# Moving steps between slots in a two-level Strassen kernel: attention's first products behind the copy of kv, sums of x earlier, last output chunk in other PSUM banks, one division into block 1

## The chip, the cores and the metric

The kernel runs on one core of one Trainium2 chip. The metric is the device time of one execution in microseconds. Timed runs have no profile; a profiled execution gives the instruction times that are read here. All data are float32.

## What is computed

A linear attention without softmax, a normalisation over each head, and a two-layer network with a leaky ReLU:

```python
kv  = einsum('bhsd,bhse->bhde', k, v)          # 8 batches, 8 heads, 576 rows, 64 wide
o   = einsum('bhsd,bhde->bhse', q, kv)
rms = sqrt(mean(o * o, axis=-1) + 1e-6)
x   = (o / rms * g_norm)                       # to (8*576, 8*64) = (4608, 512)
h   = x @ w_in                                 # (4608, 2048)
g   = maximum(0.01 * h, h)
out = g @ w_out                                # (4608, 512)
```

## The kernel before

The 4608 rows are worked in nine blocks of 512, and d_ff = 2048 in four chunks c of 2 x 256. Block 0 multiplies plainly. Block 1 uses one level of Strassen's seven products (in the Winograd form, in the order 1, 2, 6, 5, 7, 3, 4) for h and for the output. Blocks 2 to 8 use two levels for h (49 small products of 128x128) and one level for the output. The sums of the weights that the products need are made in blocks 0 and 1, kept in DRAM and read back; the sums of x and of g are made as the blocks go.

**Slots.** From block 1 on, a block is 28 slots, `slot = 7 * c + t`. A slot puts one outer product of h on TensorE (seven inner products, in banks `ha` and `hb` for one half of the inner products and `hc`, `hd` for products 2, 5, 3 of the outer level), then an attention step if the slot has one, then one product of the output (banks `oa` for products 1, 6, 7, 4 and `oc` for 2, 5, 3). The output runs two slots behind (`LAG = 2`), so slot 23 holds outer product 6 of chunk 3's h and product 1 of chunk 2's output. In `oa`, product 4 of one chunk is followed a slot later by product 1 of the next. Banks accumulate: after each product the bank is added to an SBUF tile by VectorE or copied by ScalarE (`done`), and only then may the next product write it.

**After the seventh product of h** (`product_h_two`): seven adds on VectorE make g11, g21, g22, g12 from `qa` and `qc`, four ReLUs on ScalarE (`relu`), and four sums of g on POOL (`sums_of`, in the order s1, s3, s2, s4), which the output's products 5, 7, 6, 3 need.

**Sums of x** (`sides_x`): four sums on VectorE (`sums`: t1, t2, t3, t4), then inner sums on POOL (`inner(0)`, `inner(1)`, `inner(2)`), for the next block.

**Attention** of batch i + 1 is made in block i, a step at a time (`attention`, a generator). With `fine` its 21 steps are: six for turning q and the products of kv, with q, k, v of later batches put in the load queue; one for `copy_kv` (PSUM to SBUF); and then two tails, one for the rows of the batch that end block i + 1 and one for those that begin block i + 2. A tail (`tail_of`) is: products with kv for e = 0, squares and copies on ScalarE; the same for e = 1, with two adds on VectorE; and `divide` in five steps (turn and reduce for l = 0; the same for l = 1 and the root; reciprocal and spread; turn back and multiply, twice). `FINE_SLOTS` says how many steps each slot takes, and `LATE_SLOTS` (3, 4) that the last two steps of the second tail run in the next block. Attention of batch 1 runs in block 0 with coarser steps, at the places in `steps`. Blocks 7 and 8 have no attention steps of their own; blocks 2 to 7 make sums of x for the block after.

**Order.** TensorE, transfers, and in blocks 2 to 8 VectorE's instructions are pinned to the order in which the program issues them (`pin`, `in_turn`); other instructions are placed by a scheduler. SyncE issues the loads, ScalarE the stores.

Of the kernel before, what the change touches and what calls it, by code (L numbers as in the profile page):

```python
# [23 lines left out]
def kernel(  # L24
# [46 lines left out]
    NB = B * S // NT  # L71
    N2 = NT // 2
    U = 2
    NC = DF // 2 // (U * P)
# [42 lines left out]
    def matmul(*args, **kw):  # L117
        pin(nc.tensor.matmul(*args, **kw))  # L118
# [462 lines left out]
    def add(eng, out_, a, b_, minus=False, pinned=False):  # L581
        ins = eng.tensor_tensor(out_, a, b_, op=ALU.subtract if minus else ALU.add)  # L582
        if pinned or steady and eng is nc.vector:
            pin(ins)
# [88 lines left out]
    def w_place(n):  # L673
        return view(w1_all, n % RING * NG, 7, P)
# [60 lines left out]
    def strassen(tags, left, right, done):  # L735


        banks = {}
        for i in ORDER:
            b = tags[0 if i in (1, 6, 7, 4) else 1]  # L740
            if i in FRESH:
                banks[b] = ps_m.tile([P, 2, N2], F32, tag=b, name=f"{b[0]}_{b[1]}")
            bank = banks[b]
            for part in range(2):
                for r in range(2):
                    matmul(bank[:, part, :], lhsT=left(i, part, r), rhs=right(i, part, r),
                           start=i in FRESH and part == 0 and r == 0, stop=(r == 1),
                           skip_group_check=True)
            done(i, bank.rearrange("p u (v n) -> p (u v) n", v=2))
            yield  # L750
# [4 lines left out]
    def g_of(c):  # L755


        return [view(g_all[c % 2], 0, 4, 4, P)[:, :, i, :] for i in range(4)]
# [40 lines left out]
    def product_h_two(i, c, quarters, to):  # L799

        n0 = 7 * ((i - 2) * NC + c)

        into = {1: (0, True), 2: (0, False), 6: (1, True), 5: (3, True), 7: (3, False),
                3: (1, False), 4: (2, True)}
        banks = {}
        for t, k in enumerate(ORDER):
            for js, tags, q in zip(GROUPS, (("ha", "hc"), ("hb", "hd")), (qa, qc)):
                tag = tags[0 if k in (1, 6, 7, 4) else 1]
                if k in FRESH:
                    banks[tag] = ps_m.tile([P, len(js), P], F32, tag=tag, name=f"h_{tag}")  # L810
                for n, j in enumerate(js):
                    matmul(banks[tag][:, n, :], lhsT=w_place(n0 + t)[:, AT[j], :],
                           rhs=quarters[k][j], start=k in FRESH and n == 0, stop=True,
                           skip_group_check=True)
                at, fresh = into[k]
                if fresh:
                    nc.scalar.copy(q[:, at], banks[tag])  # L817
                else:
                    add(nc.vector, q[:, at], banks[tag], q[:, at])
            read(n0 + t + 1 + RING)  # L820
            yield
        g11, g21, g22, g12 = g_of(c)
        add(nc.vector, g21, qa[:, :, 0, :], qa[:, :, 1, :])
        add(nc.vector, g11, qa[:, :, 0, :], qc[:, :, 0, :])
        yield
        add(nc.vector, g22, g21, qa[:, :, 2, :])
        add(nc.vector, g12, g22, qa[:, :, 3, :])
        add(nc.vector, g22, g22, qc[:, :, 1, :])
        add(nc.vector, g21, g21, qc[:, :, 1, :])
        add(nc.vector, g21, g21, qc[:, :, 2, :])  # L830
        for t in (g11, g12, g22, g21):
            relu(t)
        sums_of(c, to)

    def product_o(n, g_sides, os, finish):
        c = n % NC
        w_sides, _ = sides_w2(n)
        sums = sides_w2(n + 1)[1] if n + 1 < NC * (NB - 1) else lambda i: None
        if c == 0:
            for key in ("11", "12", "21", "22"):  # L840
                os[key] = opool.tile([P, 2, N2], F32, tag="o", name=f"o{key}", bufs=6)

        into = {1: ("11", True), 5: ("22", True), 2: ("11", False), 6: ("12", True),
                3: ("12", False), 7: ("22", False), 4: ("21", True)}

        def done(i, bank):
            key, fresh = into[i]
            to = os[key].rearrange("p u (v n) -> p (u v) n", v=2)
            if c == 0 and fresh:
                nc.scalar.copy(to, bank)  # L850
            else:
                add(nc.vector, to, bank, to)
            if c == NC - 1 and i in (2, 7, 3, 4):
                finish(key, os[key])

            if i == 5:
                sums(0)
            elif i == 4:
                sums(1)

        yield from strassen(("oa", "oc"), lambda i, part, r: g_sides[i][:, 2 * r + part, :],
                            lambda i, part, r: w_sides[i][:, r, :], done)

    def go(steps, n=None):
        while n is None or n > 0:
            if next(steps, steps) is steps:
                return
            n = None if n is None else n - 1
# [9 lines left out]
    def first_block(between):  # L878
# [26 lines left out]
        for t in range(4):  # L905
# [3 lines left out]
            else:  # L909
# [2 lines left out]

    first_attention()
    steps = {i: tail for tail in [tail_of(0, NT, S)] for i in (6, 8, 10)}
    steps.update((i, a1) for a1 in [attention(1, False)]
                 for i in (12, 13, 15, 16, 18, 20, 22, 23, 24, 26, 28, 29))
    loaded, rounded = 7, 5

    def between(n, half):
# [16 lines left out]
    x_sides, _, sums, _ = sides_x(1)  # L936
# [6 lines left out]
    for part in range(2):  # L943
# [1 line left out]

    A_SLOTS = (1, 3, 5, 8, 10, 11, 13, 14, 15, 17, 18, 19, 21)

    FINE_SLOTS = {1: 1, 2: 1, 4: 1, 9: 1, 10: 2, 11: 2, 12: 1, 15: 1, 16: 1, 17: 2, 18: 1, 19: 2,
                  22: 1, 24: 1, 25: 1}
    LATE_SLOTS = (3, 4)  # L950
    a_steps = iter(())

    LAG = 2
    o_queue, waited = collections.deque(), 0
# [1 line left out]
    def go_o():  # L956
        while o_queue:
            if next(o_queue[0], o_queue) is not o_queue:
                return True
            o_queue.popleft()  # L960

    for i in range(1, NB):
        one = i == 1
        steady = not one
        late, a_steps = a_steps, attention(i + 1, fine=not one) if i + 1 < B else iter(())
        os = {}
        for c in range(NC):
            g_sides = {}
            h_steps = product_h(c, h_sides, x_sides, g_sides) if one else \
                product_h_two(i, c, quarters, g_sides)  # L970
            for t in range(7):
                slot = 7 * c + t
                go(h_steps, 1)
                if not one:

                    if t == 6:
                        go(h_steps, 1)
                    if slot in LATE_SLOTS:
                        go(late, 1)
                    for _ in range(FINE_SLOTS.get(slot, 0)):  # L980
                        go(a_steps, 1)
                    if i + 1 < NB:
                        if slot == 22:
                            x_sides, new_quarters, sums, inner = sides_x(i + 1)
                        if slot in (22, 23, 24):
                            go(sums, 2 if slot == 23 else 1)
                        if slot == 24:
                            inner(0)
                        elif slot == 25:
                            inner(1)  # L990
                    load_some()
                if waited == LAG:
                    go_o()
                elif o_queue:
                    waited += 1
                if one:

                    if t == 1:
                        combine(c, 2)
                    if t == 3 and c < NC - 1:  # L1000
                        h_sides, more_h = sides_w1(c + 1)
                        combine(c + 1, 0)
                    if t == 5 and c < NC - 1:
                        more_h()
                        combine(c + 1, 1)
                    if slot in A_SLOTS:
                        go(a_steps, 1)
                    load_some()
                    if slot == 24:
                        go(a_steps)  # L1010
                        x_sides, new_quarters, sums, inner = sides_x(i + 1)
                        go(sums)
                    elif slot == 25:
                        inner(0)
                    elif slot == 26:
                        inner(1)
            go(h_steps)
            if c == NC - 1 and i + 1 < NB:
                inner(2)
                quarters = new_quarters  # L1020
            if one:
                read((2, 4, RING, RING)[c])
            o_queue.append(product_o((i - 1) * NC + c, g_sides, os, store(i)))
# [32 lines left out]
```

## Time and profile before

| | |
|---|---|
| median of 8 runs | 946.29 us (945.12 to 948.06) |
| the profiled execution | 947.4 us, span 945.7 us |
| mean granted TensorE clock | 0.996 |
| blocks 2, 3, 4, 5, 6 (237.7 to 739.3 us) | 100.3 us each |
| blocks 7, 8 | 92.1 us each |
| a plain slot | 3.29 us |

The span reaches from the first instruction to the last; about 1.7 us lie around it. In the rows of the timeline the columns are start, duration, engine, line, operation, output and inputs, shapes, count, and in brackets how long the engine had idled and what ended that. Busy time of a TensorE matmul is modelled, since matmuls are pipelined.

### The profile page before, as it was taken

The numbers are of one execution on the slowest core, as the hardware profiler recorded it, in microseconds if no ns is written. First come the engines' busy times: TensorE is split into PE (matmuls) and PEld (weight loads), VectorE is DVE, ScalarE is ACT, GpSimd is POOL, SyncE is SP. The second block draws the span as 40 slices with busy tenths as digits, with TensorE's granted clock in tenths as the row PEclk, the third lists the DMA queues.
The fourth block names the chain that finished last, engine by engine and source line by source line (L and its number), as shares of the span: only waits on it lengthen the run. The fifth ranks groups of instructions, "written<-read, shape, count | busy, mean of one in ns | idle before, by whom it ended". The sixth has DMA issues, their size and how long they took to land.

```text
span 945.7 us, 17997 instructions
## 1 busy us (share of the span) xinstructions
PE 924.0 (98%) x7076; PEld 781.1 (83%) x7076; DVE 610.9 (65%) x992; ACT 327.6 (35%) x659; POOL 320.6 (34%) x318
## 2 busy tenths in 40 slices
PE   7999999999999999999999999999999999999997
PEld 5544447878988899889988998899898999999996
DVE  2867894577456866587746874687558755754554
ACT  2543633241134322433244323432344233223321
POOL 2000353976622442226201722262224422532222
PEclk8999999999999999999999999999999999999999
DMA  7989915985498579855995589658655675567632
GB/s 249 220 228 232 256 63 189 292 294 162 147 331 261 173 202 299 265 170 182 280 280 178 181 237 300 208 176 246 229 182 167 201 220 181 182 196 222 189 110 83
DMA packets 90068, 200.05 MB, mean 212 GB/s; under 512 B 9857, under 2 KB 42113, under 8 KB 89985
## 3 DMA queue, kind: packets, MB, share of 16 engines
q1 hardware_dynamic: 79392, 186.85, 66.0%
q10 hardware_dynamic: 10144, 10.88, 3.4%
q8 instruction: 56, 0.92, 0.4%
q0 software_dynamic: 448, 1.18, 0.3%
q14 instruction: 28, 0.22, 0.1%
HBM read 172.39 MB, written 26.48 MB: 210 GB/s over the span
## 4 chain that ended last, share of the span: by engine, by line
PE 89%; DVE 6%; DMA 2%; issue 1%; ACT 0%; SPq 0%; POOL 0%; DVEq 0%; ACTq 0%; POOLq 0%
PE o_a L118 22%; PE o_c L118 18%; PE h_ha L118 10%; PE h_hc L118 8%; PE h_hb L118 7%; PE h_hd L118 6%; PE o_acc L118 4%; PE h_ps L118 4%; PE kv_ps L118 2%; PE o_ps L118 2%; PE h_a L118 2%; PE h_b L118 1%; PE h_c L118 1%; PE h_d L118 1%; DMA pairs<-in_v_dram 1%
## 5 line engine op out<-in xcount | busy, mean ns | idle before, releaser
L582 POOL TENSOR_TENSOR gs<-g 128x512 f32<-128x512 f32 x64 | 80.9, 1283 | 451.9 <-ACT g L753 451.9
L582 DVE TENSOR_TENSOR o<-o_c,o 128x512 f32<-128x512 f32 x88 | 60.6, 688 | 105.3 <-PE o_c L118 105.2
L582 DVE TENSOR_TENSOR o<-o_a,o 128x512 f32<-128x512 f32 x104 | 71.5, 688 | 86.2 <-PE o_a L118 86.2
L118 PE MATMUL o_a<-pairs,gs 128*128 128x256 f32 x512 | 121.6, 380 | 0.0
L753 ACT ACTIVATE g<-g 128x512 f32<-128x512 f32 x124 | 78.2, 631 | 116.5 <-DVE g L582 116.4
L817 ACT COPY w_all<-h_ha 128x512 f32<-128x512 f32 x84 | 48.7, 579 | 178.7 <-PE h_ha L118 176.0
L118 PEld LDWEIGHTS o_a<-pairs,gs 128*128 128x128 f32 x512 | 93.0, 190 | 11.9 <-issue 1.4
L118 PE MATMUL o_a<-w,g 128*128 128x256 f32 x256 | 61.6, 384 | 4.5 <-DVE o L582 4.5
L118 PE MATMUL o_c<-w,g 128*128 128x256 f32 x256 | 61.6, 383 | 0.0
L118 PE MATMUL o_c<-pairs,gs 128*128 128x256 f32 x256 | 61.6, 383 | 0.0
L118 PEld LDWEIGHTS h_ha<-stage,w_all 128*128 128x128 f32 x448 | 58.8, 192 | 2.9
L118 PE MATMUL o_a<-pairs,g 128*128 128x256 f32 x256 | 60.5, 379 | 0.0
L118 PE MATMUL o_c<-w,gs 128*128 128x256 f32 x256 | 60.5, 379 | 0.0
L118 PE MATMUL h_ha<-stage,w_all 128*128 128x128 f32 x448 | 59.0, 275 | 0.0
L118 PE MATMUL o_acc<-w,g 128*128 128x512 f32 x128 | 58.3, 598 | 0.7 <-ACT g L896 0.7
L118 PE MATMUL h_ps<-xT,w_all 128*128 128x512 f32 (+1 forms) x136 | 57.9, 570 | 0.2 <-DVE w_all L255 0.2
L582 DVE TENSOR_TENSOR g<-g,pairs 128x512 f32<-128x512 f32 x84 | 55.6, 689 | 1.9
L118 PEld LDWEIGHTS o_a<-w,g 128*128 128x128 f32 x256 | 46.4, 190 | 11.3 <-DVE o L582 3.4
L582 DVE TENSOR_TENSOR w_all<-h_hc,w_all 128x512 f32<-128x512 f32 x56 | 38.4, 686 | 25.4 <-PE h_hc L118 25.2
L582 POOL TENSOR_TENSOR pairs<-w_all 128x512 f32<-128x512 f32 x8 | 11.1, 1387 | 128.6 <-ACT cut L244 109.7
L118 PEld LDWEIGHTS o_c<-pairs,gs 128*128 128x128 f32 x256 | 46.4, 190 | 9.8 <-DVE inv L379 1.6
L118 PEld LDWEIGHTS o_c<-w,g 128*128 128x128 f32 x256 | 46.4, 190 | 8.6 <-issue 3.1
(188 smaller groups left out, 1964.3 us busy)
## 6 DMA issues: line engine op xcount, KB each, us to landing
w_all<-w SPq DMA_DIRECT2D x196, 448.0 KB, 4.1
pairs<-w SPq DMA_DIRECT2D x56, 512.0 KB, 4.4
out_dram<-o ACTq DMA_DIRECT2D x36, 256.0 KB, 4.5
v_in<-in_v_dram SPq DMA_DIRECT2D x29, 288.0 KB, 5.8
k_in<-in_k_dram SPq DMA_DIRECT2D x28, 288.0 KB, 5.9
q_in<-in_q_dram SPq DMA_DIRECT2D x56, 144.0 KB, 6.2
q_in<-in_q_dram SPq DMA_DIRECT2D x56, 140.0 KB, 5.8
w<-stage SPq DMA_DIRECT2D x12, 512.0 KB, 4.6
```

The lines of the kernel that those rows point to most:

```text
L118: pin(nc.tensor.matmul(*args, **kw))
L582: ins = eng.tensor_tensor(out_, a, b_, op=ALU.subtract if minus else ALU.add)
L753: nc.scalar.activation(t, t if src is None else src, func=AF.Prelu, alpha=SLOPE)
L817: nc.scalar.copy(q[:, at], banks[tag])
```

## The change

- `FINE_SLOTS`: attention's steps in blocks 2 to 6. Two steps shared slot 11 (the copy of kv and the first tail's products for e = 0); now slot 11 has the copy alone, slot 12 the e = 0 products and slot 15 those for e = 1, and the next two steps share slot 16. The second tail's e = 1 step goes from slot 19 to slot 23, and its three steps after that from 22, 24, 25 to 24, 25, 26.
- Sums of x start at slot 20 with two (before: slot 22 with one, then two, then one); the third comes in slot 21 and the fourth in slot 22. The inner sums on POOL stay at slots 24 and 25.
- The last chunk of the last block's output uses the banks `hd` and `hc` in place of `oa` and `oc`.
- `product_h_two` has one more place to pause; in the last chunk one step of the output is put there, between its second and third group of adds.
- The last step of batch 1's attention leaves block 0 and is issued in slot 4 of block 1, as the `late` part.

```diff
@@ product_h_two
         add(nc.vector, g22, g21, qa[:, :, 2, :])
         add(nc.vector, g12, g22, qa[:, :, 3, :])
+        yield
         add(nc.vector, g22, g22, qc[:, :, 1, :])
@@ product_o
-        yield from strassen(("oa", "oc"), lambda i, part, r: g_sides[i][:, 2 * r + part, :],
+        yield from strassen(("oa", "oc") if n + 1 < NC * (NB - 1) else ("hd", "hc"), lambda i, part, r: g_sides[i][:, 2 * r + part, :],
@@ block 0
-    steps.update((i, a1) for a1 in [attention(1, False)]
-                 for i in (12, 13, 15, 16, 18, 20, 22, 23, 24, 26, 28, 29))
+    a_steps = attention(1, False)
+    steps.update((i, a_steps)
+                 for i in (12, 13, 15, 16, 18, 20, 22, 23, 24, 26, 28))
@@ blocks 1 to 8
-    FINE_SLOTS = {1: 1, 2: 1, 4: 1, 9: 1, 10: 2, 11: 2, 12: 1, 15: 1, 16: 1, 17: 2, 18: 1, 19: 2,
-                  22: 1, 24: 1, 25: 1}
+    FINE_SLOTS = {1: 1, 2: 1, 4: 1, 9: 1, 10: 2, 11: 1, 12: 1, 15: 1, 16: 2, 17: 2, 18: 1, 19: 1,
+                  23: 1, 24: 1, 25: 1, 26: 1}
...
-    a_steps = iter(())
...
-                        if slot == 22:
+                        if slot == 20:
                             x_sides, new_quarters, sums, inner = sides_x(i + 1)
-                        if slot in (22, 23, 24):
-                            go(sums, 2 if slot == 23 else 1)
+                        if slot in (20, 21, 22):
+                            go(sums, 2 if slot == 20 else 1)
...
+                    if slot == 4:
+                        go(late, 1)
                     if slot in A_SLOTS:
...
+            if i == NB - 1 and c == NC - 1:
+                go(h_steps, 1)
+                go_o()
             go(h_steps)
```

## The prediction

> **What bounds the kernel now.** I read the page first, then TensorE's waits from the first two-level block on, then the length of every slot (one h product and one o product, with attention products in some), and last the other engines' timeline around the slots that are too long.
>
> ```profile
> span 945.7 us, 17997 instructions
> ...
> PE 924.0 (98%) x7076; PEld 781.1 (83%) x7076; DVE 610.9 (65%) x992; ACT 327.6 (35%) x659; POOL 320.6 (34%) x318
> ```
>
> TensorE is busy 98% of the span: only its holes can be won. Waits of TensorE from 237 to 945 us (total, times, longest):
>
> ```profile
> PE o_ps L118 <- DVE kv L321: 5.0, 5, 1.0
> PE o_a L118 <- DVE o L582: 4.5, 6, 2.1
> ```
>
> Five waits of 1.01 us are attention's first products waiting for the copy of kv, one in each of blocks 2 to 6. The o_a waits are five of 0.48 us in the same blocks and one of 2.07 us at the end. A hole costs more than its wait, so I take slot lengths, from one h product's start to the next. A plain slot is 3.29 us (417.88 to 421.17). In block 3, slots 11, 12, 22 and 23, of 28 counted from 0 (stretch, then length and busy times):
>
> ```profile
> 377.05:382.40 5.35, 4.34 (x39) 3.50 (x38) 2.32 (x5) 1.39 (x4) 0.00 (x0) 1.00 1.05 288
> 382.40:386.48 4.08, 4.08 (x40) 3.34 (x39) 1.99 (x4) 1.97 (x5) 0.00 (x0) 1.00 0.80 245
> 417.88:421.17 3.29, 3.29 (x24) 3.08 (x23) 3.22 (x7) 1.66 (x4) 1.50 (x2) 1.00 0.46 145
> 421.17:425.20 4.03, 3.55 (x23) 3.15 (x22) 4.03 (x5) 1.06 (x2) 3.95 (x3) 1.00 0.80 246
> ```
>
> Slots 11 and 12 hold equal attention products (64x256), yet differ by 1.27 us; over the five blocks the pairs are 5.46/4.18, 5.35/4.08, 5.25/3.97, 5.14/3.86 and 5.04/3.75: 6.40 us in all. Slot 23 holds no attention and is 4.03 or 4.04 instead of 3.29: 0.75 x 5 = 3.7 us. Why it is long (timeline):
>
> ```profile
> 420.90 1.26 POOL L582 TENSOR_TENSOR gs<-g 128x512 f32<-128x512 f32 x1
> ...
> 421.45 1.27 DVE L582 TENSOR_TENSOR xt<-xT 128x512 f32<-128x512 f32 x1
> 422.13 1.72 POOL L582 TENSOR_TENSOR gs<-gs,g 128x512 f32<-128x512 f32 x1
> ...
> 422.64 0.68 DVE L582 TENSOR_TENSOR o<-o_a,o 128x512 f32<-128x512 f32 x1
> ...
> 423.37 1.99 PE L118 MATMUL o_a<-w,g 128*128 128x256 f32 x8 [0.48 <-DVE o L582]
> ```
>
> VectorE's first sum of x takes 1.27 us, where it took 0.69 with POOL idle (225.85 us, block 1). It ends 0.55 us after POOL's second sum of g (its s3), and then comes the add that frees bank o_a. The same holds in all of blocks 2 to 6: it starts 0.85, 0.72, 0.59, 0.45 and 0.33 us before s3 ends and lasts 1.40, 1.27, 1.14, 1.00 and 0.87 us.
>
> **The change part by part.** In the changed program's instruction order, everything up to slot 11 of block 2 is the same on every engine, and SyncE's queue is the same throughout. Work, operations and transfers are unchanged.
>
> *Division into block 1.* The scheduler put that division's instructions at the same places before. Worth 0; no DMA moves.
>
> *First products a slot later.* The copy of kv stays in slot 11 (done 379.83), attention's e=0 products go to slot 12 (at 382.40 - 2.06 for the shorter slot 11 + 1.65 into the slot = 382.0): no wait can be left. The e=1 products go to slot 15. Slot 11 falls to 3.29: -(26.24 - 16.45) = -9.79; slot 12 keeps its length with the other half's products; slot 15 grows from 3.29 to slot 12's lengths, +(19.84 - 16.45) = +3.39. Sum **-6.40**. Behind the e=1 products ScalarE has two squares and two copies, then the copy of o_a that slot 16's product needs: from the products' start to the last copy 2.16 us (384.05 to 386.21), so until 3.8 us of slot 15. Bank o_a is filled at 4.2, its copy ends at 4.8, and slot 16 wants the bank at 5.6. Cover 0.8 us; if it is gone, 0.1 to 0.5 us a block.
>
> *Sums of x two slots earlier, and the second tail's e=1 products from slot 19 to slot 23.* In slot 20 VectorE now runs g21, g11 (413.07, 413.68), the first two sums at 414.29 and 415.01 (0.61 and 0.72 later, as in block 1), then the add of o at 415.62 instead of 414.79, since it had idled 0.42 us there. All after it is 0.83 us later: the last three g adds at 417.74, POOL's sums of g at 420.50, its s3 from 421.73 to 423.00. The third sum runs at 419.68 to 420.37, just ahead of POOL: no cost. But the fourth, in slot 22, starts at 419.68 + 0.61 + 0.60 + 0.59 + 0.47 = 421.95, inside s3. By the five rows it ends 0.55 after s3: 423.55. The add of o ends at 424.15, slot 23's o product starts at 424.20. So the same collision remains, with another sum, 0.83 us later. Slot 23 becomes 4.04 + 0.83 = 4.87; the attention products now in it (4.08 to 4.50 as slot lengths) fit in the hole. Slot 19 falls from 21.46 in total to 16.45. Sum over five blocks: +4.15 - 5.01 = **-0.86**. Block 7 has sums of x but no attention to fill the hole; its slot 23 was 3.29 and becomes 4.87: **+1.58**.
>
> Here a rule of the Trainium skill bears. *SBUF — State Buffer*, "Who interferes with whom": a VectorE instruction with two SBUF inputs contends with a GpSimd instruction that reads SBUF; the loser blocks until the other's whole instruction is over. The rows agree in kind. Taken at its worst (a whole POOL sum of 1.28 ahead of 0.69), the fourth sum would end at 423.92, 0.37 later: 6 x 0.37 = 2.2 us more. I keep the rows' 0.55.
>
> VectorE's two e=1 adds in slot 23 also meet POOL; even with a POOL sum of 1.28 each, the add of o after them is done by about 428.6 and bank o_a is wanted in slot 25, at 430.9. POOL's inner sums of x still wait for slot 24's products to leave their buffer, and POOL has room (34%). The second tail's turning and reciprocal move from slots 22, 24, 25 to 24, 25, 26, where the sums of x have left VectorE free.
>
> *Last chunk in banks of h, and the added yield.*
>
> ```profile
> 925.87 2.02 DVE L582 TENSOR_TENSOR g<-g,pairs 128x512 f32<-128x512 f32 x3
> ...
> 927.81 0.68 DVE L582 TENSOR_TENSOR o<-o_c,o 128x512 f32<-128x512 f32 x1
> ...
> 928.63 2.48 POOL L582 TENSOR_TENSOR gs<-g 128x512 f32<-128x512 f32 x2 [17.95 <-ACT g L753]
> ...
> 929.24 1.97 PE L118 MATMUL o_a<-w,g 128*128 128x256 f32 x8 [2.07 <-DVE o L582]
> ...
> 931.07 1.27 POOL L582 TENSOR_TENSOR gs<-gs,g 128x512 f32<-128x512 f32 x1
> ...
> 932.76 0.59 PE L118 MATMUL o_a<-pairs,gs 128*128 128x256 f32 x2
> ```
>
> The bank wait of 2.07 goes: products 1 and 2 can start at 927.01 and 928.74. Product 6 then wants POOL's s2 at 930.47. In the new order the o_c add stands ahead of the last three g adds: 0.60 later for them, for the ReLU, for POOL; s2 ends at 932.94 instead of 932.34. Product 6 starts about 933.0 instead of 932.76, plus 0.10 of restart (an o product after a wait takes 1.83, not 1.73): **+0.35**. No row shows how fast TensorE follows POOL; bounds -0.1 (it starts before POOL's recorded end) and +0.7; nearest is 0.05, its start after VectorE. A rule speaks otherwise: *Perfetto Trace Analysis*, "Optimizing Tensor Performance", wants independent groups in different PSUM banks so that evacuation overlaps the next matmuls; by it 2.2 us would be won here and the whole sum be -7.9. The rows say that POOL's chain ends last, so I take +0.35.
>
> **Sum:** -6.40 - 0.86 + 1.58 + 0.35 = -5.3 us against the profiled execution (947.4, span 945.7 and 1.7 around it). That run lies 1.1 above the median of eight, 946.29; holes in a program order do not depend on that, so I take the difference to the median: **941.0**.
>
> **The rivals.**
> *The fourth sum slips in ahead of s3.* It is only 0.22 us late for that (421.95 against 421.73). Then it ends by 422.6, the o product follows at 423.3, and slot 23 has no hole in blocks 2 to 6: -3.73 instead of -0.86, and block 7 pays 0.64: -6.40 - 3.73 + 0.64 + 0.35 = -9.1, **937.2**. Against it: both chains start from the same g add, so their distance is rigid. 0.13.
> *Partly eaten:* the skill's whole-instruction block, or slot 15's ScalarE cover gone: 1.5 to 2.5 us less, **942.5 to 943.5**. No row shows it. 0.09.
> *Slower: POOL takes the port twice.* If s2 goes before the waiting fourth sum, six slots 23 grow by another 1.28: 941.0 + 7.7 = **948.7**. It decides from 5.3/6 = 0.89 us a block. Against it: in all five rows VectorE went in after the instruction under way, and s2 was stretched to 1.72. With a few unforeseen queues at that place, 0.05.
> *No change* (the gain eaten in slots 20 to 23 almost exactly): 0.03.
>
> **How the numbers follow.** My case has 0.70, with its own range 939.9 to 942.2 (end bound, slot 15). To hold 8 in 10 the range takes in the early slip below and the eaten part above: 937.0 to 943.3. A difference of 0.2% (1.9 us) is about what a measurement of this kernel can tell from none. Faster by more: 0.70 + 0.13 + 0.09 = 0.92; within: 0.03; slower: 0.05.
>
> **What the changed profile would show.** Right: no wait of o_ps on kv; slot 11 at 3.29; slot 23 near 4.9 in blocks 2 to 7, with a wait of o_a on VectorE's o and a fourth sum of about 1.6 us that ends after s3; at the end no bank wait, but product 6 waiting for POOL's gs. Wrong: slot 23 at 4.1 to 4.5 (early slip), or over 5.7 (POOL twice); a new wait in slots 12, 15 or 16; a last product 6 that starts at once.

## The result, and the profile after

| | before | after |
|---|---|---|
| median | 946.65 us (32 runs, 944.72 to 948.37) | 942.38 us (11 runs, 940.53 to 944.69) |
| ratio, 95% interval | | 0.9957 (0.9949 to 0.9966) |
| the profiled execution | 947.4 us, span 945.7 | 943.18 us, span 941.5 |

The change makes the kernel 0.43% faster: 4.1 us (3.2 to 4.8 by the interval), where 5.3 were forecast. The difference is larger than the noise, and smaller than the forecast by more than the noise. The head of the page after:

```profile
span 941.5 us, 17989 instructions
...
PE 923.0 (98%) x7076; PEld 781.0 (83%) x7076; DVE 616.0 (65%) x992; ACT 327.1 (35%) x659; POOL 317.6 (34%) x318
```

VectorE is busy 5 us longer with the same 992 instructions: some of them now stand longer beside POOL. TensorE's waits from 237 to 945 us (total, times, longest):

```profile
PE o_a L118 <- DVE o L582: 4.1, 6, 1.3
PE h_d L118 <- POOL gs L582: 2.3, 1, 2.3
PE o_a L118 <- ACT o L851: 0.6, 1, 0.6
```

The five waits for the copy of kv are gone. Three others stand there instead: slot 23 (six times, the longest in block 7), product 6 of the last chunk behind POOL, and one on ScalarE, in block 6, which the forecast had named as a danger and put at nothing in its sum. The slots of block 3 that answer to those shown before, in the order 11, 12, 22, 23, then slot 23 of blocks 4 and 7 (stretch, length, busy times of TensorE, weight load, VectorE, ScalarE and POOL with the number of instructions, granted clock, busy share of the DMA engines, GB/s):

```profile
374.22:377.51 3.29, 3.29 (x24) 3.08 (x23) 2.31 (x5) 0.00 (x0) 0.00 (x0) 1.00 0.98 272
377.51:381.58 4.07, 4.07 (x39) 3.34 (x38) 1.23 (x2) 1.97 (x5) 0.00 (x0) 1.00 0.92 296
...
412.88:416.17 3.29, 3.29 (x24) 3.08 (x23) 3.22 (x6) 2.63 (x5) 0.33 (x1) 1.00 0.48 142
416.17:421.38 5.21, 4.25 (x39) 3.34 (x38) 5.21 (x7) 2.66 (x6) 5.13 (x4) 1.00 0.73 257
515.38:520.24 4.86, 4.36 (x39) 3.34 (x38) 4.67 (x6) 2.88 (x6) 4.78 (x4) 1.00 0.80 271
807.29:812.14 4.85, 3.56 (x23) 3.16 (x22) 2.96 (x4) 1.06 (x2) 4.76 (x4) 1.00 0.79 262
```

Slot 11 is plain. Slot 23 is 4.86 where the forecast had 4.87, and 5.21 in block 3. The timeline of block 4 shows the collision in its new place:

```profile
514.71 2.50 POOL L582 TENSOR_TENSOR gs<-g 128x512 f32<-128x512 f32 x2 [20.22 <-ACT g L753]
...
516.15 1.60 DVE L582 TENSOR_TENSOR w_all<-xT,w_all 128x512 f32<-128x512 f32 x1
517.17 1.72 POOL L582 TENSOR_TENSOR gs<-gs,g 128x512 f32<-128x512 f32 x1
517.68 0.68 DVE L582 TENSOR_TENSOR o<-o_a,o 128x512 f32<-128x512 f32 x1
...
518.41 1.99 PE L118 MATMUL o_a<-w,g 128*128 128x256 f32 x8 [0.50 <-DVE o L582]
```

POOL's s1 and s3 (first line) end at 517.21. The fourth sum of x (second line; in this block t4 lies in a `w_all` tile) starts inside s3 and ends about 0.55 us after it: it takes 1.60 us where 0.69 is its price alone, and the add that frees o_a can only follow it.

Slot lengths before and after, all blocks:

| slots | before | after | difference | forecast |
|---|---|---|---|---|
| 11, blocks 2 to 6 | 5.46, 5.35, 5.25, 5.14, 5.04 | 3.29 each | -9.79 | -9.79 |
| 15, blocks 2 to 6 | 3.29 each | 4.19, 4.08, 3.97, 3.87, 3.75 | +3.41 | +3.39 |
| 16, block 6 | 3.29 | 4.11 | +0.82 | 0 |
| 19, blocks 2 to 6 | 4.08, 4.19, 4.29, 4.40, 4.50 | 3.29 each | -5.01 | -5.01 |
| 23, blocks 2 to 6 | 4.04, 4.03, 4.04, 4.04, 4.04 | 4.86, 5.21, 4.86, 4.86, 4.86 | +4.46 | +4.15 |
| 23, block 7 | 3.29 | 4.85 | +1.56 | +1.58 |
| slot 0 of block 2 to slot 27 of block 8 | 682.53 | 677.98 | -4.55 | -5.68 |

Two parts of the span lie outside that table. The start, to slot 0 of block 2, is 1.58 shorter in the profile after (237.73 to 236.15). That is not the change. In both profiles the instructions of TensorE, VectorE, ScalarE and POOL come in the same order up to slot 11 of block 2. And over all the profiles of this document, the four with the division at its old place (before, and the three parts tried alone) have that slot at 235.7 to 237.7, on average 236.6, and the nine with the new place at 235.7 to 237.6, on average 236.8. The end, from slot 27 of block 8, is 1.93 *longer* (25.44 to 27.37), where +0.35 was forecast. Its rows, in stretches (columns as above):

```profile
924.33:926.74 2.41, 0.16 (x1) 0.00 (x0) 0.69 (x1) 0.00 (x0) 2.36 (x2) 1.00 0.23 81
926.74:928.50 1.76, 1.76 (x4) 1.49 (x5) 0.00 (x0) 0.00 (x0) 1.26 (x1) 0.51 0.11 38
928.50:930.26 1.76, 1.76 (x6) 1.37 (x6) 0.00 (x0) 0.00 (x0) 0.00 (x0) 0.52 0.00 0
930.26:931.98 1.72, 1.72 (x9) 1.52 (x8) 0.69 (x1) 0.00 (x0) 0.00 (x0) 1.00 0.00 0
```

Product 6 starts at 926.74, after 2.41 us without a product, and then runs at half the clock: 3.68 us instead of 1.9. Before, TensorE stood still for 2.23 us two products earlier, ahead of product 1, and went on at full clock. Whether the change causes that, or an execution happens to draw it, no single trace can tell.

### The profile page after: what moved, and what is told of

Its sections match the earlier page's. It is cut to its first block, busy times and chain, and to the rows that moved or that the text cites. A ratio compares the mean times of both kernels' runs of the same rounds, so it can differ in the third digit from the quotient of the medians.

```text
span 941.5 us, 17989 instructions
## 1 busy us (share of the span) xinstructions
PE 923.0 (98%) x7076; PEld 781.0 (83%) x7076; DVE 616.0 (65%) x992; ACT 327.1 (35%) x659; POOL 317.6 (34%) x318
## 3 DMA queue, kind: packets, MB, share of 16 engines
q0 software_dynamic: 448, 1.18, 0.3%
## 4 chain that ended last, share of the span: by engine, by line
PE 87%; DVE 8%; DMA 2%; issue 1%; POOL 1%; ACT 1%; SPq 0%; ACTq 0%; DVEq 0%; POOLq 0%
PE o_a L118 21%; PE o_c L118 17%; PE h_ha L118 10%; PE h_hc L118 8%; PE h_hb L118 7%; PE h_hd L118 6%; PE o_acc L118 4%; PE h_ps L118 4%; PE kv_ps L118 2%; PE o_ps L118 2%; PE h_d L118 2%; PE h_c L118 2%; PE h_a L118 1%; DMA pairs<-in_k_dram 1%; DVE o L582 1%
## 5 line engine op out<-in xcount | busy, mean ns | idle before, releaser
L582 DVE TENSOR_TENSOR o<-o_c,o 128x512 f32<-128x512 f32 x85 | 58.5, 688 | 108.2 <-PE o_c L118 108.1
L118 PE MATMUL o_a<-pairs,gs 128*128 128x256 f32 x496 | 117.3, 379 | 0.0
L582 DVE TENSOR_TENSOR o<-o_a,o 128x512 f32<-128x512 f32 x100 | 68.7, 687 | 71.1 <-PE o_a L118 71.0
L118 PEld LDWEIGHTS o_a<-pairs,gs 128*128 128x128 f32 x496 | 90.0, 190 | 9.9
L118 PE MATMUL o_c<-w,g 128*128 128x256 f32 x248 | 59.7, 383 | 0.0
L118 PE MATMUL o_c<-pairs,gs 128*128 128x256 f32 x248 | 59.2, 381 | 0.0
L118 PEld LDWEIGHTS o_a<-pairs,g 128*128 128x128 f32 x248 | 45.0, 190 | 6.5 <-DVE w_all L582 0.9
```

## The experiments

Each is a kernel with one edit, timed against the kernel before on the same chip. "Start to end" below is from slot 0 of block 2 to slot 27 of block 8, so it holds neither the start nor the end.

**The copy of kv alone** (in the kernel before):

```diff
-    FINE_SLOTS = {1: 1, 2: 1, 4: 1, 9: 1, 10: 2, 11: 2, 12: 1, 15: 1, 16: 1, 17: 2, 18: 1, 19: 2,
+    FINE_SLOTS = {1: 1, 2: 1, 4: 1, 9: 1, 10: 2, 11: 1, 12: 1, 15: 1, 16: 2, 17: 2, 18: 1, 19: 2,
```

> Only attention's first products are moved (e=0 from slot 11 to 12, e=1 from 12 to 15); sums of x, the last chunk's banks and the division stay as in the kernel before. If the forecast's first step holds: slot 11 at 3.29 in blocks 2 to 6 (-9.79), slot 15 at 4.19 to 3.75 (+3.4), and the ScalarE wait that the changed kernel showed in block 6 (0.8) may come back: -5.6 to -6.4, about 940.5 against 946.4. Slots 19 and 23 as in the kernel before. The rival, that the copy of kv was only hiding a later wait (ScalarE's copies in slot 15 in every block): -3 to -4, with a wait of o_a on ScalarE in slot 16 of all five blocks.

Measured: 941.82 us, ratio 0.9953 (0.9940 to 0.9965), so about -4.5 us; the median is 1.3 above the one expected. Start to end is -5.50, just short of what was expected: slot 11 falls to 3.29 to 3.35 in all five blocks, slot 15 is 4.18 to 3.76, and block 6's slot 16 is 4.12, +0.83. The wait on ScalarE in block 6 belongs to this part, then; blocks 2 to 5 have none. The profile's last chunk ran its product 1 at half clock (3.51 us), and two of the five executions had a mean granted clock of 0.995, where none of the 30 of the kernel before, timed beside them, was under 0.996. The three executions at 0.996 have a median of 941.52, the 19 of the kernel before at 0.996 one of 947.28: -5.8, near what the slots say. This part alone gives all of the gain.

**The sums of x and the second tail alone** (in the kernel before):

```diff
-... 18: 1, 19: 2, 22: 1, 24: 1, 25: 1}
+... 18: 1, 19: 1, 23: 1, 24: 1, 25: 1, 26: 1}
-                        if slot == 22:
+                        if slot == 20:
-                        if slot in (22, 23, 24):
-                            go(sums, 2 if slot == 23 else 1)
+                        if slot in (20, 21, 22):
+                            go(sums, 2 if slot == 20 else 1)
```

> Only the sums of x (slots 20 to 22) and the second tail's e=1 products (slot 19 to 23) are moved. The forecast's step: the fourth sum of x takes 1.6 us and ends 0.55 after POOL's third sum; slot 23 at 4.87 in blocks 2 to 6 (+0.83 each) and in block 7 (+1.58), slot 19 at 3.29 (-5.01): together +0.7, up to +1.1 with the odd longer slot of block 3, so about 947.2 (no gain). The rival, that moving the sums is what makes the changed kernel faster: -3 to -4, 942.5, with no hole in slot 23.

Measured: 948.30 us, ratio 1.0020 (1.0010 to 1.0030): a loss of 1.9 us (0.9 to 2.8). Start to end +0.99, slot by slot as in the table above (slot 23 at 4.85, 5.22, 4.86, 4.86, 4.86; block 7 4.84). The rival's gain is not there. The slots' +0.99 lies at the lower end of that interval. The rest lies with the clock: seven of the 17 executions had a mean clock under 0.996, where none of the 30 before had. At equal clock the medians differ by 0.9 (0.996: 948.15 of 7 and 947.28 of 19) and 1.3 (0.998: 946.98 of 3 and 945.68 of 11). Why this kernel had the low clock so often stays open.

**The end alone** (in the kernel before): the added `yield`, the banks `hd` and `hc`, and the o product put ahead.

> Only the last chunk's output goes to the banks of h, with the yield and the o add put ahead. POOL's chain ends last: product 6 waits 2.2 us for POOL's sums of g instead of 2.07 for the bank earlier. The forecast's +0.35 if TensorE then runs at full clock; +1.9 if the half clock (0.51) of the changed kernel comes back in product 6 after that wait. The rival (independent banks are won in full): -2.2.

Measured: 947.09 us, ratio 1.0007 (0.9997 to 1.0016): no difference that this can tell. TensorE's waits, in total, times, longest:

```profile
PE h_d L118 <- POOL gs L582: 2.2, 1, 2.2
```

Product 6 waits for POOL exactly as in the changed kernel, 12.61 after slot 27 in both, but here it runs at full clock, 2.00 us. From slot 27 to the end of the span it is 25.67, +0.23 to before. At equal clock the medians say the same: +0.2 at 0.998 (4 and 11 executions), +0.3 at 0.996 (9 and 19). So +0.35 was the right size; the other 1.7 of the profile after is the half clock, and the half clock does not always come. The -2.2 that the bank rule would have given did not come: the bank was free, and the product waited for its operand.

**Filling the gap.** Matmuls of 128x512 into bank oa between products 2 and 6, in the changed kernel, with results that are never read: five (below), and later two.

```diff
+            if i == 2 and n + 1 == NC * (NB - 1):
+                fill = ps_m.tile([P, NT], F32, tag="oa", name="fill_ps")
+                for _ in range(5):
+                    matmul(fill, lhsT=w2_sb[0][c][:, 0, :P], rhs=w2_sb[0][c][:, 0, :], start=True, stop=True)
```

> The changed kernel with five matmuls of 128x512 added into bank oa, between the last chunk's output products 2 and 6; their result is never read. They shorten the idle stretch of TensorE there from 2.4 us to about 1.2. If the idle stretch is what halves the clock: product 6 starts at the same distance behind POOL and takes 1.9 us instead of 3.7, so -1.75 against the changed kernel (940.7). If the half clock has another cause (the last work of the kernel, POOL's traffic, the length of the run): no change, or the half clock stays.

Measured: 943.26 us, ratio 0.9967 (0.9955 to 0.9979). I had sized it badly: the five took 4.45 us, not 1.2, so product 6 started 14.49 after slot 27 instead of 12.61. It ran at full clock (1.89), and what was won so was lost by the later start.

> The changed kernel with two matmuls of 128x512 (1.8 us by the 4.45 of the five tried) in the gap ahead of the last chunk's product 6; their result is never read, and product 6 starts as before, 12.6 after slot 27. If an idle TensorE is what halves the clock there: never a halved product 6, so no execution at a mean clock of 0.994, and a median 0.5 to 1.7 below the changed kernel's 942.4. If the halving has another cause, executions at 0.994 go on turning up and the median stays.

Measured: 942.68 us, ratio 0.9958 (0.9946 to 0.9971). Two took 1.88, product 6 started 12.62 after slot 27 and ran 1.99, and none of five executions had a mean clock of 0.994 (four of twelve of the changed kernel had). But the expected lower median did not come: four of the five had 0.996, as with two half-clock stretches at the start. As a test of the cause by the time it is inconclusive.

**The fourth sum of x early** (in the changed kernel):

```diff
-                        if slot in (20, 21, 22):
-                            go(sums, 2 if slot == 20 else 1)
+                        if slot in (20, 21):
+                            go(sums, 2)
```

> The changed kernel, with the third and the fourth sum of x both in slot 21, so that the fourth is done before POOL's third sum of g starts. If slot 23's hole is that one collision: slot 23 is as long as its attention products need (4.08 to 4.50 instead of 4.86, and 5.22 in block 3), about -3.2 in blocks 2 to 6, and about -0.9 in block 7: 938.3 against 942.4 for the changed kernel. If another instruction of VectorE takes the fourth sum's place behind POOL, or the add of o is late for another reason, slot 23 stays near 4.86 and the time near 942.4.

Measured: 938.17 us, ratio 0.9914 (0.9902 to 0.9927). Slot 23 is 4.08, 4.30, 4.29, 4.39, 4.50, and 3.92 in block 7; start to end -4.01 against the changed kernel. Block 4 in its timeline:

```profile
513.86 0.68 DVE L582 TENSOR_TENSOR w_all<-xT,w_all 128x512 f32<-128x512 f32 x1
514.08 2.83 POOL L582 TENSOR_TENSOR gs<-g 128x512 f32<-128x512 f32 x2 [20.23 <-ACT g L753]
...
516.12 0.68 DVE L582 TENSOR_TENSOR o<-o_a,o 128x512 f32<-128x512 f32 x1
516.87 1.26 POOL L582 TENSOR_TENSOR gs<-gs,g 128x512 f32<-128x512 f32 x1
```

The fourth sum (first line) takes 0.68, the o_a add is done before POOL's s2 (last line) starts, and TensorE waits for neither. So the hole of slot 23 in blocks 2 to 6 was that one collision. In block 7 0.63 of 1.56 remain, with a wait of 0.4 for the o_a add.

**The root a slot later** (in the changed kernel). The step that moves holds one turn and one reduce on VectorE, and the root on ScalarE:

```diff
-    FINE_SLOTS = {... 15: 1, 16: 2, 17: 2, 18: 1, 19: 1,
+    FINE_SLOTS = {... 15: 1, 16: 1, 17: 3, 18: 1, 19: 1,
```

> The changed kernel, with the second half of the sums' turning and the root of attention's division in slot 17 instead of 16, so that in block 6 ScalarE copies bank o_a ahead of the root. If the 0.55 wait in block 6 comes from that order: slot 16 of block 6 at 3.29 again, -0.82 and nothing else. If the division is then late for the second tail's products: a new wait or longer slots from 18 on, and no gain.

Measured: 941.88 us, ratio 0.9949 (0.9937 to 0.9962). Block 6's slot 16 is 3.29 again (-0.82), and slot 23 of block 3 is 4.86 instead of 5.21 (-0.35), which I had not foreseen. Start to end is -1.18. The medians of the two kernels (941.88 and 942.38) are too close to show that; the slot lengths do.

**The end without the o product put ahead, and POOL's chain made longer** (both in the changed kernel). The first leaves out `go(h_steps, 1)` and `go_o()` at the end; the second does POOL's first sum of g twice in the last chunk:

```diff
         add(nc.gpsimd, s1, g21, g22)
+        if twice:
+            add(nc.gpsimd, s1, g21, g22)
```

> The changed kernel without the o add put ahead at the end, so that the last three g adds, and POOL's sums behind them, come 0.60 earlier. Product 6 should start 12.0 after slot 27 instead of 12.6, with a gap of 1.8 us. The reading of the half clock so far: it is decided at the ends of 3.41 us stretches, and set for the next one when TensorE stood still for more than about 2.1 us of one; a gap of 1.8 then never halves it. So -0.6, and -2.3 against executions whose product 6 was halved: median about 941.2, no execution at 0.994, product 6 at 1.9 to 2.0. If any gap of that size can halve the clock, product 6 may take over 3 us and executions at 0.994 turn up. If the o add ahead is what lets product 6 start, it is later and the time goes up.

Measured: 941.90 us, ratio 0.9941 (0.9927 to 0.9955). Product 6 starts 12.15 after slot 27 (-0.46), after a gap of 1.95, runs 1.99, and no execution of six had a mean clock under 0.996. The median fell by 0.5, less than the 1.2 expected.

> The changed kernel, with POOL's first sum of g done twice in the last chunk (same operands and result), so that its chain is one sum (1.25) longer and the gap 3.66 us. If POOL's chain sets product 6: +1.25 in every execution. By the reading of the 3.41 us stretches, a gap of 3.66 leaves more than 2.1 us in one stretch in about eight of ten phases, so that product 6 is mostly halved (+1.75 there): median about +2, 944.3, most executions at 0.994 or 0.996. If POOL's chain had slack: no change.

Measured: 945.18 us, ratio 0.9979 (0.9967 to 0.9991). Product 6 starts 13.94 after slot 27 (+1.33) and runs at half clock, 3.57. POOL's chain has no slack there. Six of twelve executions had a mean clock under 0.996, where four of twelve of the changed kernel had. The median is 2.8 above the changed kernel's, more than the start of product 6 alone makes and more than the 2 expected.

**What is best of all that.** Fourth sum early, root in slot 17, with the two unread matmuls in the gap:

> The changed kernel with all three: fourth sum of x early, root in slot 17, two unread matmuls in the last gap. If the three causes are separate, their gains add: -4.1 - 0.8 - 0.7 from 942.4, about 936.8; against the kernel before about -10. If one of them only uncovers the next, less.

Measured: 936.89 us, ratio 0.9894 (0.9879 to 0.9909). And without them, with the o product not put ahead:

> The changed kernel with the fourth sum early, the root in slot 17, and the end without the o add ahead in place of the unread matmuls. If the gains add: -4.1 (sums), -0.8 (root), -0.6 to -1.4 (end) from 942.4, about 936.3; 0.5 below the one with the unread matmuls. If the earlier g adds only move the wait: as that one.

Measured: 936.47 us, ratio 0.9884 (0.9866 to 0.9902), beating both kernels. Its waits of TensorE from 237 to 940 us:

```profile
PE h_d L118 <- POOL gs L582: 1.8, 1, 1.8
PE o_a L118 <- DVE o L582: 0.4, 1, 0.4
```

Of 11 waits in the kernel before, two are left. The gains nearly add up: start to end is 673.02, -4.96 to the changed kernel (-4.01 and -1.18 alone).

## Why the prediction was right, point by point

**The sum.** 5.3 us were forecast and 4.1 (3.2 to 4.8) came. The slots between start and end say -4.55, and the end, at equal clock, +0.23: -4.3. The parts tried alone say the same: -5.50 + 0.99 + 0.23 = -4.3. So about 1.0 of the forecast is missing, and it has two places, both of them losses: nothing cancelled by luck. The median, 942.38, lies in the forecast's wide range (937.0 to 943.3), but 0.2 above the range that its main case gave itself (939.9 to 942.2). All its signs of being right came, and one of its signs of being wrong: a new wait in slot 16.

**First products a slot later (-6.40): right in slots 11 and 15 to 0.02, short by one wait of 0.82.** The step that failed is "Cover 0.8 us; if it is gone, 0.1 to 0.5 us a block". The cover held in blocks 2 to 5 and failed in block 6, where the products are only 64 wide. I had read ScalarE's order behind the products as two squares, two copies, then the copy of o_a. In block 6 the root stands between (rows of the timeline):

```profile
686.57 2.49 POOL L582 TENSOR_TENSOR gs<-g 128x512 f32<-128x512 f32 x2 [19.81 <-ACT g L753]
687.41 1.74 DVE L353 TENSOR_TENSOR sum<-sum,sq 128x64 f32<-128x64 f32 x2
...
689.99 0.30 ACT L367 ACTIVATE rms<-rms,eps_sb 128x4 f32<-128x4 f32 x1 [2.37 <-DVE rms L364]
690.20 0.56 ACT L851 COPY o<-o_a 128x512 f32<-128x512 f32 x1
...
690.81 1.99 PE L118 MATMUL o_a<-w,g 128*128 128x256 f32 x8 [0.55 <-ACT o L851]
```

ScalarE's order is not pinned, and in block 6 alone of the five the root stands ahead of the copy of o_a; what led the scheduler to that is not known. The root waits for VectorE's two adds, which now fall beside POOL's sums of g and take 1.74 us together (0.36 in the kernel before); ScalarE idles 2.37, and the copy of o_a, whose bank had long been full, waits behind it. With the root's step one slot later, the copy of o_a stands first (688.70 in that profile) and the 0.82 is gone, while VectorE's two adds still take 1.75: the order on ScalarE is the cause. The forecast read ScalarE's queue in one block, block 3, with products 256 wide, and took it for all five.

**Sums of x (-0.86, and +1.58 in block 7): right in mechanism, and in size but for block 3.** The collision remained with the fourth sum, which ends 0.55 behind POOL's s3, slot 23 at 4.86 for 4.87, block 7 +1.56 for +1.58. The rule of the Trainium skill taken at its worst, *SBUF — State Buffer*, "Who interferes with whom" (a whole POOL instruction of waiting), would have made these slots 0.37 longer; in the rows VectorE waits only for the rest of the instruction under way. Missing is 0.35 in block 3: there the g add in slot 20 starts as ScalarE's *second* copy ends (VectorE's wait before it is 1.24 where block 4 has 0.89, and there the add starts as the *first* copy ends), and everything behind it is late by that. It is there in all six kernels in which the third and fourth sums stand in slots 21 and 22 and the root in slot 16, and it went with the root's move to 17. Why that add waits for the second copy stays open.

So this half of the change, meant or not, is a loss by itself (+0.99): slot 23 pays almost all that slot 19 saves, and block 7 pays for nothing.

**The end (+0.35): right, with the profile after misleading.** At equal clock it is +0.23. The bank's wait went and POOL's chain took its place, product 6 at +0.1 of where it had been; that chain has no slack (one more sum: +1.33).

**Division into block 1 (0).** No run isolates it, but the start shows no effect: on average 236.6 in four profiles with the old place and 236.8 in nine with the new one, where the profiles of one group differ by up to 2.1.

**The rivals.** The fourth sum did not slip in ahead of s3 by itself; put there by hand it gave 4.0, where that rival's sum had 3.8 more (941.0 to 937.2), and block 7 kept 0.63 of its loss, where the rival's sum left 0.64. In every slot 23 of blocks 2 to 7 the fourth sum went in after s3 and ahead of s2: the slower case is not in any trace. The partly eaten case is the nearest to what happened, with the ScalarE wait that it named, in one block instead of five.

## What to carry to other kernels

When a step is moved next to another, read the queue of every engine it feeds in the *smallest* case as well: a short instruction can be placed ahead of one that a bank waits for, and its own wait then becomes the bank's, as when ScalarE sat idle for 2.37 us ahead of the root here. A collision between VectorE and POOL is not gone because the work was moved earlier; it is gone when the last of the adds is done before POOL's instruction starts, and here one more sum in the slot before was worth as much as the whole change. A gap of 2.2 us or more in TensorE had to be costed twice here: as its own length, and as a chance of running the next 3.4 us at half clock.

## What the runs showed of the hardware that was not expected

**The half clock at the end begins and ends on a grid of 3.413 us that does not start with the kernel.** In every profile TensorE runs at half clock for one or two stretches early in the start-up. In the profile after, these end at 22.25 us, and the half clock at the end begins at 926.75: 904.50 later, or 265 x 3.4132. In four other profiles with a half-clocked product at the end, the same two moments lie 264 (20.8 to 921.9, and 23.35 to 924.45), 265 (21.65 to 926.15) and 266 (21.0 to 928.95) times 3.413 apart, and each ends on the next line of the grid. Continuing each profile's own grid gives the stretch that holds most of the gap. Here are that stretch and the next one, first with only kv moved, then with only the sums moved. Both have the same gap of 2.23 us and the same wait of 2.07:

```profile
918.50:921.91 3.41, 1.34 (x7) 0.89 (x6) 2.98 (x5) 1.69 (x3) 0.85 (x1) 1.00 0.39 89
921.91:925.32 3.41, 3.41 (x9) 2.73 (x9) 0.11 (x1) 0.00 (x0) 3.33 (x4) 0.50 0.16 65
```

```profile
925.37:928.79 3.42, 1.50 (x7) 0.97 (x6) 3.35 (x6) 1.89 (x3) 0.46 (x1) 1.00 0.27 49
928.79:932.20 3.41, 3.26 (x15) 2.94 (x16) 0.69 (x1) 0.00 (x0) 3.33 (x4) 1.00 0.26 105
```

```profile
921.66 3.51 PE L118 MATMUL o_a<-w,g 128*128 128x256 f32 x8 [2.07 <-DVE o L582]
```

```profile
928.94 1.97 PE L118 MATMUL o_a<-w,g 128*128 128x256 f32 x8 [2.07 <-DVE o L582]
```

The third and fourth fence are the products behind those gaps, in the same order. In the first, TensorE was busy 1.34 of the 3.41 us and the next stretch has clock 0.50; in the second the gap reaches over the line, TensorE was busy 1.50, and the clock stays. All profiles without unread matmuls; in each, product 6 or product 1 of the last chunk follows a gap (moments of the grid are read to 0.05 us):

| kernel | gap | TensorE busy in the stretch with most of the gap | product after it |
|---|---|---|---|
| longer POOL chain | 3.75 | 0.04 | 3.57, half |
| fourth sum early | 2.41 | 1.15 | 3.17, half from 924.45 on |
| changed kernel | 2.41 | 1.16 | 3.68, half |
| root later | 2.41 | 1.16 | 3.51, half |
| kv alone | 2.23 | 1.34 | 3.51, half |
| sums alone | 2.23 | 1.50 | 1.97 |
| best, no unread matmuls | 1.95 | 1.68 | 1.99 |
| before | 2.23 | 2.11 | 1.97 |
| end alone | 2.41 | 2.25 | 2.00 |
| o product not ahead | 1.95 | 2.26 | 1.99 |

So at this place the limit lies between 1.34 and 1.50 busy, or 39 and 44% of a stretch. For a gap of 2.2 to 2.4 us it is then the phase of the execution that decides; no experiment here set the phase, so this rests on the agreement of the ten profiles. It is not a rule for other work. In the start-up, where the matmuls are others, TensorE is busy for 2.01 us (changed kernel) and 1.54 us (root later) in the last stretch ahead of the half clock. With the sums alone, a stretch with 1.93 us is followed by full clock. The three stretches, in this order:

```profile
12.00:15.41 3.41, 2.01 (x31) 0.87 (x24) 0.00 (x0) 0.00 (x0) 0.00 (x0) 1.00 0.66 199
14.83:18.24 3.41, 1.54 (x72) 1.35 (x72) 0.00 (x0) 1.25 (x2) 0.00 (x0) 1.00 0.68 169
7.16:10.57 3.41, 1.93 (x75) 1.80 (x69) 1.55 (x4) 1.25 (x2) 0.00 (x0) 1.00 1.02 391
```

Busy time alone does not decide there; what does is open. The Trainium skill, *TensorE: Matmul & The Clock Gate*, "Part 1: The HAM clock gate", has the free-running window of 3413 ns, and these moments agree; it names an idle window as what halves the clock, while these runs show that a window busy to 39% can be enough.

One such stretch costs about 1.7 us (product 3 follows product 6's start by 3.52 in the changed kernel, by 1.83 with the end alone), and the mean clock of an execution counts them: in the set timed beside the first four experiments, 11 executions of the kernel before with a clock of 0.998 have a median of 945.68, 19 with 0.996 one of 947.28. So a good part of what scatters between executions of one kernel here is how many such stretches they draw, but not all: those at 0.998 still lie between 944.65 and 948.43. A difference of one execution against one other is therefore uncertain by 1.7 us from this alone, some four tenths of the gain that was measured.
